# Two of the five subtractions that make wv's low parts: on VectorE instead of GpSimd, with the written-out order of TensorE's products made anew

## The chip, the core and the metric

The kernel runs on one core of a Trainium2 chip. The metric is the device time of one execution in microseconds, as the median of several runs. Before the change it is 1871.93 us (three runs, 1871.77 to 1875.42).

## The reference

x is 2048 rows of 640 numbers, float32 throughout. The output is the sum of x, an attention block and a token-mixing MLP, both fed with the layer norm of x:

```python
xn = layernorm(x)
qkv = xn @ wqkv                      # 32 heads of 20
o = softmax(q @ k.T * 20 ** -0.5) @ v
A = o @ wo
h = gelu(layernorm(xn) @ w1)         # then shifted by +1, -1, +2, -2 rows, a quarter of the columns each
x1 = xn + shifted(h) @ w2
B = x1 + gelu(layernorm(x1) @ w3) @ w4
out = x + A + B
```

## The kernel before, in words

**Numbers in two parts.** To keep float32 precision on TensorE, an operand is split into a high part (a rounded copy in the fp32r type) and a low part (the operand minus its high part). A product is three: high by high, high by low, low by high. The high part is a copy, mostly on ScalarE; the low part is a subtraction, on GpSimd or VectorE. A pair of such products that uses the two 64-row halves of the array side by side is called twins here; between the first and the second half of a twin sum stands a fence, a one-element memset of `scratch` on GpSimd, which waits for the last product of the first half and releases the first of the second.

**The first stage** (to about 30 us) loads x in 16 tiles (`xb`), takes the mean and variance of each on VectorE (`bn_a`, `mva`), works out the norm's factors in short steps on GpSimd (`rv_a` is VectorE's, then `rn_a`, `ry_a` which is the power -0.5, `rt_a`, and `lnk` at the end), scales the tiles (`xb` again, on VectorE and ScalarE in turn), transposes them on TensorE (`tp`) and splits the result into `xT` (high copy on ScalarE, low subtraction on VectorE). Tiles go in groups: 0 and 1, 2 and 3, then 4 to 7, 8 to 11, 12 to 15. For each block of four tiles the products with the first 128 columns of the q and k weights (`w_q`, `w_k`, sums named `ps`) follow, their split `hl`, and a placing product `pk`. The first half of the v weights (`wv`, five pieces of 128 x 320, one per 128 rows) and `w_k`, `w_q` (128 x 640 each) are split in the same stretch. Their subtractions are tied behind the scaling of tile 2 on VectorE. After the five pieces of wv, GpSimd has the subtractions of `w_k` and `w_q`, four memsets of the buffers `vst` (which held the raw v weights), and the norm factors of the next block.

**After the first stage** the attention (maxima `pm` and `mx`, scores `s`, exponentials `p`, weighted sums `pv`) runs through the whole kernel, and the dense products (v, q, k, w1 to w4, wo) fill in between.

**What sets the order.** The program lists operations with keys (smaller is more urgent) and costs; a planner walks through them in modelled time and emits one order for each engine. The engines then work in that order. For TensorE the kinds are written out in the string `ORDER` of 7059 letters: m a maximum step, s a score step, p a weighted sum, d anything else; which d comes is still chosen by key. Operations marked `port=True` are kept apart in the plan: no such operation of VectorE overlaps one of GpSimd there. That holds in the modelled time alone; on the chip only the order on each engine and the waits for data stand.

Nearly all vector, scalar and GpSimd instructions are recorded at L324 (the line in `Plan.__call__` that issues them), products at L356, fences at L344.

Of the kernel before, what the change touches and what calls it, by code (L numbers as in the profile page):

```python
# [97 lines left out]
ORDER = (  # L98
    "dddddddddddddddddddddddddddddddddddddddddddddddddddddddddddddddddddddddddddddddddddddddddddddddddddddddddmmddd"
    "ddddddddddddddddddddddddddddddddddddddddddddddddddddddddddddmdddddddmddddmddddmddddmddddddmdddddddddddddddmddd"  # L100
    "dddmmdddddddmdddddmddddddddmdmddddddddddddddddddmdddddddddmdmmdddddddddddddddmdddddddddddmddddmmdddddddddddddd"
    "mdddddmddddddddmdddmmdddddddddddddddddddddmddddddddmdmmdddddddmddddddddddddddddddddmddmddmdddddddmdddddddddddd"
    "mdddddddddddsmmdddddddddddsddsdddddddsdmdddddddddmssddddddddmdsdddsdddmdddddsdmdsddppppddmsddmddsdmdsddsddmdds"
    "dddsdmdmddppppmddddmsdddsddddmdsdddsmdddsdmdsddddsmddsddmddmmppppmdsdddsdsdmdddmdsddmdddsmddddsdmddsdmddsddmdm"
    "ddmdpppsmspsmsmspmsmpsmspmsmpsmssmpmsmpsmddddsmddddmdddsdmdddsmdddsdmdddsdmddsdmddmddsppssmpsmmppmdddsddmddsdd"
    "dmddddmdspddmsdddddsdmdsdddddmddmppsmddddddddsmdddddddsmdddddsddmdddsddddmdmppmsdddddsddmdsddddmdddsmddddddsdm"
    "ddddsdddmdmppppsmddddsddmddsddddsdddmsddddddmsddddmdddddsmpmsmpppdsmdddsddddddmsdddddsmddddsddmddsdddmdddmdspp"
    "ppdmdsmdddddddsddmdddddmsddddddmsdddsdddmdddmppsdmdddddsdmddddsddmddsdmdddsdddmddsdddddmdmppsmdddddsdmddsddddd"
    "ddmsmdddddddsddddmddmddmppmsmppmdsdsdddmdsddddmsdddddmmsdddddddmsdddsddmsdddsppmspsmsddpdssmpdddppsddsddmdddsd"
    "ddsdmddddsmdddmddsdddmddsddmdddsppmmspppdmsddddmsdddsdmdsdddddmsmdddsdddmdsddsdddmddmdsppmsmsppmsdddmmpdpdsmdd"  # L110
    "ddmdsdddmddsddmddsdmdsdddmdsdddsddmddsddspsmpmspdmspdppdmdsddmddddmddddsdddsmddsddmddsdddsmdsddmddsdmppppmsddm"
    "dddddmsdddmdsdmdddsmddddmsdddmddsdmdddsddmppsmmppmsddddsdsmddddsdmddsdddmsddmddsdmdddspsmpsdmdddmdsddddsmppdmm"
    "sdpdpsdddsdsdddddmsddddsdddmsddddmdsddddmdsdddmddsppmmsmspppsmspsmddddmdsdmdddmddsddddmsdddmsddddmsdddmdsdddmd"
    "mppssppsmdddddpssmpmdddsdmdddsdmdddsddddsmddddmdsdddmdddsddsddmpppmsmpdddsmddddmddmddsdddddmsddddmdsddddmsdddd"
    "ddsmsmpsmpppsmspsddmdpmdsddmdsdddmsdddddmssdddddmddmdsddsddmddsdpsmmpppsdmddddsmdsdddmdsddmddsdsppppmsdddmsddd"
    "msdddmdsddmdddssdddddpsmmppmddsdmddmdddddsdmpdmsdddsdmsdddmdsddmddsdmdddsddsdmppppmsdddmdsddsddsdmddddddmsmddd"
    "ddddsmddddmsddsddmsmmpppmspsmspsmddddsmdddsdmpsmddddmddsdmdsddddmspsdmpsmdddsdddmsddsdmdddddmddsppppddsmddsddm"
    "dddsmddsddmdsdmddsddmdsdmddmdmppppssddmddddmsdddmdsdddddmsmddddsddmdddsmdddsddmdmppppmsddmdsdddmdsddmddsddmdds"
    "mdddmdsdddsdsddmpsmpsmpsmpmsddmdsddddsdddsdmdmdpppdsddmddsdddsmpmsddmdsddmdsdddsddmsdddmdsppsmmppmsdddmdsddmdd"
    "ddmdsddddmsmdddddsmddddmdsdddmddspsmmpppmdddmddsdddmsddddmsdddmsddmdsdddmddmsddddsdmddspmspssmpsmspsmsdpsmspms"  # L120
    "mpmspssmpssmpssmpmsspsmpssmpsmmppmsddddmddddmdddddddmmdddddsdddddddddddddddmsddsddddddddssdddmddddddmdsdddddsd"
    "dddmdmppppmdddsdddddddsmdmddddddsddmddddsdddddddddddddddsddddddddddddmsmddddddsddddmddddddddsddmddddddmddddspp"
    "ppdmdsddddsddddmsddddsdddddddddddddsdddddsdddmsddddddmmdddddddsdddmdddmddppdsppmdddddsdmddsddddddsmdsddddddsdd"
    "mdddddsdmppsdmddddddsdmdddddsddmpdmsddddddmddsddddddmspsmpsmspssmppsddddddddddddddddddddsspmmspsmmppmmddsddddd"
    "dmdddmsddddsmdmddddddmsdddmdsdddmddddmdsddmdddmsdddmddddsmddddmdsdmddddspppppmsdddddddmddsddmddsddmddsdddsmddd"
    "sddmddsddsddmddddmmppppmsdddmdddddsdmddsdmdddsmdddsdmdddsdmdddsdmdddsmpppmsdddsdmdsdddmdsdddmsdddsmdsddddmmppp"
    "msdpsmddsddmdsddmddsdmpppsmdddsdmdddsdmdddsdmdddsmdddsdmddsdmddsdmddsdddmmppppmdddmddddsddmddsddddssdddmdddsds"
    "ddmdddsddsdspppsmspmmsppsmdddsdmdddsdmdddsdmdddsmdddsdmdddsddmddsdddmdspdppmsddmdsdddmsddmdsddmdsdddmmppppmsdd"
    "sddmdsdddmdsdmdddsdddddmddddmmdddddddsmdppsdmdddsdmddsddsddmdddsdmpsmspssmppppmsddmdsddddmsdmdddsddmddsmdddsdm"
    "ddddsmddsddmdddmsppppdmdsdmdddsdmdddmdsdddddssmdddddsddmddsdmdddddsmmmppmpmmspsmspsmspsmspsmspsmspsmspssmpmsmp"  # L130
    "ddddsmdddmdddsdddddsmdddsdddmddmppsmdddddddddddsdddsdddmdddddsmddddddddsdddmddddddddsdddddmdddspmddsdpdsmdsddd"
    "ddddmddddmmdddddddddddddpppddmdddddddsddddddsmddddddmddddmdddddspsmdddsddddmddsddsddddmsdddddmddsdddmdddsddddd"
    "dddddddppppmsdddddmsddddsdmdddddsmdddddmsdddmddddddmdspmsppddmsdddddddmsddddddsdmddddddsdmddddddmdspdmdsddmddd"
    "ddsddddddmmdddddsddddddsddddmsppdmsmppsmspssmpmsspmsspmsddddddddssddddddddddddpmspssmpsmspsmspsmspsmdddddsspps"
    "sddddmdsddddmdmmddddddmdddmdddddddddmdddddmdddddddmsdddmdddmddddmdsddmdddddmddmddddmdsdddddmmddddsddmddsdppdmd"
    "dsddddmmpppmddsddmdddddmddsdmdddsmdddsdmddsdmddsdmddsddmdsppsmspppsmdddsdmdddsdmdddsdmdddsmdddsddmddsddmddsdds"
    "ddmpppssmpppmsddsddmddsddmddsdmddddsmdsdddmddsdmddddsmddddmsppppddmdmdddsddddsdmdsddddmsddmddsdsddddmsdddmdmdd"
# [448 lines left out]
def c_act(n, psum=True):  # L586
    return n * 0.8333 + (50.0 if psum else 93.0)
# [6 lines left out]
def c_pool(n):  # L594
    return 2.11 * n + 145.0
# [6 lines left out]
def _f(v):  # L602
    return v.bitcast(F32)


def tile_kernel(tc, x, wqkv, wo, w1, w2, w3, w4, out):
    nc = tc.nc
    pl = Plan(tc)
# [192 lines left out]
    wvs, nbs, rvs = [], [], []  # L801
# [17 lines left out]
    def v_load(h):  # L819
        vp = pl.pool(name=f"vw{h}", bufs=1, side="right")  # L820
        w = vp.tile([P, 2, ND, 320], F32R, name=f"wv{h}")
        for k in range(ND if h else 0):
            load_row(w, "v1", k, 1)
        return vp, w
# [4 lines left out]
    vw0 = v_load(0)  # L829
    vst = [vsp.tile([P, 8, 2, VC], F32, name=f"vst{i}") for i in range(VSB)]  # L830
    wvr = [v.rearrange("p a b c -> p (a b c)")[:, :320] for v in vst]
# [9 lines left out]
    def split_wv():  # L841
        k, pl.key = pl.key, -903.0
        for i in range(ND):
            pl("act", c_act(320, False), "copy", vw0[1][:, 0, i, :], wvr[i])
            wvs.append(pl("pool", c_pool(320), "tensor_sub", vw0[1][:, 1, i, :], wvr[i], _f(vw0[1][:, 0, i, :]), port=True))
        pl.key = k

    pl.key = -140.0
# [2 lines left out]
    def norm_rows(ts):  # L851
# [30 lines left out]
        if ts[0] == 0:  # L882
            split_wv()
# [681 lines left out]
```

## Time and profile before

| | |
|---|---|
| median of three runs | 1871.93 us (1871.77 to 1875.42) |
| the profiled execution's own time | 1870.62 us |
| its span, first to last instruction | 1868.5 us |
| TensorE busy | 1855.8 us, 99% of the span |
| VectorE busy | 1550.7 us, 83% |
| ScalarE busy | 1337.8 us, 72% |
| GpSimd busy | 404.8 us, 22% |
| granted TensorE clock, mean | 0.999 |

The profiled execution lies 2.1 us above its span and 1.3 us below the median. In the tables PE is TensorE's products, PEld its weight loads, DVE is VectorE, ACT is ScalarE, POOL is GpSimd. Busy time is an average over stages; what an edit in one stage is worth is read from that stage.

### The profile page before, as it was taken

Reading aid. Unit: us, or ns where it says so; the run is one execution under the profiler, and the core shown is the slowest. Engines: PE = TensorE matmul, PEld = TensorE weight load, DVE = VectorE, ACT = ScalarE, POOL = GpSimd, SP = SyncE. Lnnn points to the kernel's source line nnn. Section 1 sums busy time; section 2 is a strip of 40 time slices with the busy share of each in tenths; the row PEclk is TensorE's granted clock in tenths of the full one; section 3 lists DMA queues with packets and bytes.
Section 4 is the critical chain, followed back from the end, with each engine's and each line's share of the span. In section 5 each row is a group of like instructions: output and inputs, shape, how many; then the busy total and the mean of one; then the engine's idle time right before and its main releaser. Section 6 shows DMA issues by size and latency. Waiting matters only on the chain.

```text
span 1868.5 us, 44324 instructions
## 1 busy us (share of the span) xinstructions
PE 1855.8 (99%) x17233; PEld 1276.6 (68%) x17233; DVE 1550.7 (83%) x2739; ACT 1337.8 (72%) x2459; POOL 404.8 (22%) x620
## 2 busy tenths in 40 slices
PE   9999999999999999999999999999999999999998
PEld 7975776666666648676666756665776777775777
DVE  8989888888888999988788988778887888789724
ACT  5267777787877886677887677788677777778661
POOL 6001111321212213211213320111222122212211
PEclk9999999999999999999999999999999999999999
DMA  5664555536353475645345673434423242343402
GB/s 200 178 184 134 136 136 158 162 115 180 107 158 122 123 243 169 189 151 177 118 127 187 210 208 102 126 98 151 121 80 91 73 116 84 81 135 121 139 13 113
DMA packets 230360, 257.79 MB, mean 138 GB/s; under 512 B 60520, under 2 KB 175672, under 8 KB 228352
## 3 DMA queue, kind: packets, MB, share of 16 engines
q1 hardware_dynamic: 230152, 254.98, 45.7%
q8 instruction: 135, 2.21, 0.5%
q14 instruction: 73, 0.60, 0.1%
HBM read 151.64 MB, written 103.25 MB: 136 GB/s over the span
## 4 chain that ended last, share of the span: by engine, by line
PE 95%; DVE 2%; POOL 1%; DMA 1%; issue 0%; SPq 0%; ACT 0%; DVEq 0%; POOLq 0%; ACTq 0%
PE ps L356 26%; PE pv L356 25%; PE s L356 14%; PE pm L356 14%; PE psv L356 4%; PE pso L356 3%; PE ps_k L356 3%; PE ps_q L356 3%; DVE mx L324 1%; PE psl L356 1%; PE tz L324 1%; DMA wd_w<-ph_w 0%; PE pmt L356 0%; PE c_w L356 0%; PE tp L324 0%
## 5 line engine op out<-in xcount | busy, mean ns | idle before, releaser
L324 DVE TENSOR_REDUCE mx<-pm 128x1 f32<-128x512 f32 x2048 | 1282.2, 683 | 207.9 <-PE pm L356 192.9
L324 ACT ACTIVATE p<-s 128x512 f32<-128x512 f32 x2048 | 1080.8, 611 | 277.4 <-PE s L356 232.7
L356 PE MATMUL pv<-p,v 128*32 128x512 f32 x4096 | 493.7, 598 | 0.1
L356 PE MATMUL s<-zq,kpack 62*128 62x512 f32 x2048 | 443.4, 410 | 0.7
L356 PE MATMUL pm<-kpack,zq 60*128 60x512 f32 x2048 | 441.0, 409 | 1.6 <-DVE ob L324 1.6
L356 PE MATMUL ps<-xT,w_w 64*128 64x512 f32 x2040 | 322.8, 394 | 0.4 <-DVE mx L324 0.3
L356 PEld LDWEIGHTS s<-zq,kpack 62*128 62x128 f32 x2048 | 227.4, 185 | 128.2 <-ACT p L324 38.6
L356 PEld LDWEIGHTS pm<-kpack,zq 60*128 60x128 f32 x2048 | 228.3, 185 | 110.6 <-DVE mx L324 26.3
L356 PEld LDWEIGHTS pv<-p,v 128*32 128x32 f32 x4096 | 110.2, 109 | 225.0 <-issue 196.1
L356 PEld LDWEIGHTS ps<-xT,w_w 64*128 64x128 f32 x2040 | 212.9, 186 | 32.9 <-issue 2.1
L324 POOL TENSOR_TENSOR ob<-ob,obq 128x512 f32<-128x512 f32 x96 | 125.2, 1304 | 403.2 <-ACT obq L324 312.3
L356 PE MATMUL ps<-xT 64*128 64x320 f32 x1632 | 168.0, 307 | 0.0
L356 PEld LDWEIGHTS ps<-xT 64*128 64x128 f32 x1632 | 150.2, 186 | 9.0 <-issue 2.5
L356 PE MATMUL ps<-xT,gT 64*128 64x320 f32 x1152 | 119.1, 307 | 0.0
L324 ACT COPY obq<-pv 128x512 f32<-128x512 f32 x75 | 44.1, 588 | 103.8 <-PE pv L356 102.8
L356 PEld LDWEIGHTS ps<-xT,gT 64*128 64x128 f32 x1152 | 104.4, 186 | 6.2 <-issue 0.8
L344 POOL MEMSET scratch<- 1x1 f32 x134 | 12.1, 90 | 432.0 <-PE ps L356 206.3
L356 PE MATMUL psv<-wv,xT 64*128 64x320 f32 x960 | 92.1, 309 | 1.0 <-ACT xT L324 0.8
L356 PEld LDWEIGHTS psv<-wv,xT 64*128 64x128 f32 x960 | 80.9, 185 | 7.4 <-POOL scratch L344 1.2
L356 PE MATMUL ps_q<-xT,w_q 64*128 64x512 f32 x480 | 77.9, 393 | 0.0
L356 PE MATMUL ps_k<-xT,w_k 64*128 64x512 f32 x480 | 74.4, 394 | 0.0
L324 POOL TENSOR_TENSOR ph_w<-pr_w,ph_w 128x320 fp32r<-128x320 f32 (+2 forms) x48 | 36.7, 764 | 151.6 <-ACT ph_w L324 120.9
(171 smaller groups left out, 1360.9 us busy)
## 6 DMA issues: line engine op xcount, KB each, us to landing
zq<-qd SPq DMA_DIRECT2D x156, 80.0 KB
kpack<-kd SPq DMA_DIRECT2D x78, 160.0 KB
w_w<-wd_w SPq DMA_DIRECT2D x48, 256.0 KB
gd<-pre SPq DMA_DIRECT2D x8, 1536.0 KB
g<-gd SPq DMA_DIRECT2D x64, 192.0 KB
wd_w<-ph_w SPq DMA_DIRECT2D x34, 320.0 KB
xT<-wd_w SPq DMA_DIRECT2D x34, 320.0 KB
vd<-vst SPq DMA_DIRECT2D x32, 256.0 KB
```

The costliest lines, as they stand in the source:

```text
L324: o.insts = [getattr(e, m)(val(out), *[val(x) for x in ins], **{k: val(v) for k, v in kw.items()})]
L344: o.insts = [nc.gpsimd.memset(scratch.get(), 0.0)]
L356: o.insts = [nc.tensor.matmul(out.get(), lhsT.get(), rhs.get(), **kw) for out, lhsT, rhs, kw in products]
```

## The change

In `split_wv`, which lists the five copies and five subtractions for wv's parts, the subtractions of pieces 2 and 4 are now listed for VectorE, with VectorE's cost in the planner; pieces 0, 1 and 3 stay on GpSimd. Key, tie and marking are as before. None of the five may be moved to another engine by the planner. The string ORDER is another one of the same length with the same number of each letter. Counted letter by letter, 77 of its 1024 m, 78 of its 1024 s and 11 of its 512 p stand elsewhere, by 23 places at most, in 32 stretches; the first 232 letters are the same. The core of the diff:

```diff
--- before
+++ after
@@ -98,40 +98,40 @@
 ORDER = (
...
-    "dddmmdddddddmdddddmddddddddmdmddddddddddddddddddmdddddddddmdmmdddddddddddddddmdddddddddddmddddmmdddddddddddddd"
-    "mdddddmddddddddmdddmmdddddddddddddddddddddmddddddddmdmmdddddddmddddddddddddddddddddmddmddmdddddddmdddddddddddd"
-    "mdddddddddddsmmdddddddddddsddsdddddddsdmdddddddddmssddddddddmdsdddsdddmdddddsdmdsddppppddmsddmddsdmdsddsddmdds"
-    "dddsdmdmddppppmddddmsdddsddddmdsdddsmdddsdmdsddddsmddsddmddmmppppmdsdddsdsdmdddmdsddmdddsmddddsdmddsdmddsddmdm"
-    "ddmdsdddmddsddmddsdmdsdddmdsdddsddmddsddspsmpmspdmspdppdmdsddmddddmddddsdddsmddsddmddsdddsmdsddmddsdmppppmsddm"
-    "dddddmsdddmdsdmdddsmddddmsdddmddsdmdddsddmppsmmppmsddddsdsmddddsdmddsdddmsddmddsdmdddspsmpsdmdddmdsddddsmppdmm"
+    "dddmmddddddddmddddmdddddmddddmddddddddddddddddddmdmdddddddddmmddddddddddddddmddddddddddddmddddmmdddddddddddddd"
+    "mdddddmddddddddmdddmmddddddddddddddddddddddmdddmdddddmmddddddddddddmdddddddddddddddmdddmdddddddmdddddddddddddm"
+    "ddddmdddddddsmddddmddddddsddsddddddddsddsdmdddddddmsddddsddmdddsdddmdddddsdmppppdsddsdddmdmdddsddmsdddsddddmds"
+    "dddsdmdmddppppmddddmdsddsdddsdmddddsmddsdddmsddddsmddsddmddmmppppdmsddsddsdmdddmdsdmddddsmddddsdmddsdmddsddmdm"
+    "ddmdsdddmddsddmddsdmdsdddmdsdddsddmddsddspsmpmspdmspdppdmdsddmddddmddddsdddsmddddsmddsdddsmdsddmddsdmppppmsddm"
+    "ddddmsdddmdsddmdddsmddddmdsddmddsdmdddsddmppsmmppmsddddsdsmddddsdmddsdddmsddmddsdmdddspsmpsdmdddmdsddddsmppdmm"
...
@@ -842,7 +842,9 @@
         k, pl.key = pl.key, -903.0
         for i in range(ND):
             pl("act", c_act(320, False), "copy", vw0[1][:, 0, i, :], wvr[i])
-            wvs.append(pl("pool", c_pool(320), "tensor_sub", vw0[1][:, 1, i, :], wvr[i], _f(vw0[1][:, 0, i, :]), port=True))
+            on = i in (2, 4)
+            wvs.append(pl("dve" if on else "pool", (c_dve if on else c_pool)(320), "tensor_sub", vw0[1][:, 1, i, :], wvr[i],
+                          _f(vw0[1][:, 0, i, :]), port=True))
         pl.key = k
 
     pl.key = -140.0
```

## Rows read from the trace of the kernel before

**Rows 1.** The page, part 1: busy time and share of the span, by engine.

```profile
PE 1855.8 (99%) x17233; PEld 1276.6 (68%) x17233; DVE 1550.7 (83%) x2739; ACT 1337.8 (72%) x2459; POOL 404.8 (22%) x620
```

**Rows 2.** Stretches: from:to, length, busy us and instructions by engine, clock, DMA share, GB/s.

```profile
10.00:30.00 20.00, 17.41 (x141) 13.27 (x141) 18.56 (x49) 12.02 (x23) 14.42 (x31) 1.00 0.67 249
30.00:60.00 30.00, 30.00 (x240) 24.75 (x238) 27.22 (x56) 12.36 (x23) 6.20 (x13) 1.00 0.33 111
```

**Rows 3.** Chain that ended last, 0 to 160 us: start us, us, what.

```profile
...
13.37 2.56 POOL wv L324 x3
15.93 1.54 POOL w_k L324
17.47 1.50 POOL w_q L324
...
19.61 0.97 POOL ry_a L324
...
23.96 0.91 ACT xb L324
...
25.49 1.29 DVE hl L324 x2
26.78 1.80 DVE xT L324 x3
28.63 3.71 PE ps L356 x29
...
```

**Rows 4.** GpSimd in order of time: start us, us, instruction, idle before it.

```profile
...
11.71 3.40 POOL L324 TENSOR_TENSOR wv<-vst,wv 128x320 fp32r<-128x320 f32 x4 [0.51 <-ACT xT L324]
...
20.98 0.09 POOL L344 MEMSET scratch<- 1x1 f32 x1
...
22.90 0.20 POOL L324 TENSOR_TENSOR lnk<-rn_a,lnk 128x4 f32<-128x4 f32 x1
23.05 1.30 POOL L324 TENSOR_TENSOR ry_a<-rv_a,mhalf 128x4 f32<-128x4 f32 x1
...
25.55 0.20 POOL L324 TENSOR_TENSOR lnk<-rn_a,lnk 128x4 f32<-128x4 f32 x1
...
```

**Rows 5.** VectorE in order of time, 10.9 to 19 us.

```profile
...
11.49 1.62 DVE L324 TENSOR_TENSOR xT<-tp,xT 128x512 fp32r<-128x512 f32 x3
...
18.77 0.22 DVE L324 SCALAR_TENSOR_TENSOR rv_a<-mva 128x4 f32<-128x4 f32 x1
...
```

**Rows 6.** TensorE in order of time: its two waits for GpSimd after 18 us.

```profile
...
19.03 0.50 PE L356 MATMUL ps<-xT,w_q 64*128 64x512 f32 x1 [0.81 <-POOL w_q L324]
...
21.13 0.50 PE L356 MATMUL ps<-xT,w_q 64*128 64x512 f32 x1 [0.68 <-POOL scratch L344]
...
```

**Rows 7.** VectorE, groups by form: busy us, mean ns, idle before.

```profile
...
L324 DVE TENSOR_TENSOR ph_w<-pr_w,ph_w 128x320 fp32r<-128x320 f32 x10 | 4.9, 490 | 0.9 <-ACT ph_w L324 0.7
...
```

**Rows 8.** Both engines in order of time, two places late in the kernel.

```profile
...
1786.66 0.68 DVE L324 TENSOR_TENSOR oT<-oc,oT 128x512 fp32r<-128x512 f32 x1
...
1786.82 1.67 POOL L324 TENSOR_TENSOR oT<-oc,oT 128x512 fp32r<-128x512 f32 x1 [4.30 <-DVE oT L324]
...
1817.44 1.30 POOL L324 TENSOR_TENSOR ob<-ob,obq 128x512 f32<-128x512 f32 x1 [5.54 <-ACT obq L324]
...
1818.11 1.18 DVE L324 TENSOR_TENSOR oTl<-oc,oTl 128x512 fp32r<-128x512 f32 x1
...
1831.88 0.69 DVE L324 TENSOR_TENSOR oTl<-oc,oTl 128x512 fp32r<-128x512 f32 x1
...
```

**Rows 9.** Chain that ended last, where TensorE changes to weighted sums and back.

```profile
...
107.66 3.57 PE pv L356 x32
...
156.57 1.00 PE pv L356 x8
157.56 0.42 PE pm L356 x2
158.22 0.24 PE pm L356 x2
...
```

More of the change, by code (lines that the diff above doesn't have):

```diff
@@ L110 @@
     "ddsdmddddsmdddmddsdddmddsddmdddsppmmspppdmsddddmsdddsdmdsdddddmsmdddsdddmdsddsdddmddmdsppmsmsppmsdddmmpdpdsmdd"
-    "ddmdsdddmddsddmddsdmdsdddmdsdddsddmddsddspsmpmspdmspdppdmdsddmddddmddddsdddsmddsddmddsdddsmdsddmddsdmppppmsddm"
-    "dddddmsdddmdsdmdddsmddddmsdddmddsdmdddsddmppsmmppmsddddsdsmddddsdmddsdddmsddmddsdmdddspsmpsdmdddmdsddddsmppdmm"
+    "ddmdsdddmddsddmddsdmdsdddmdsdddsddmddsddspsmpmspdmspdppdmdsddmddddmddddsdddsmddddsmddsdddsmdsddmddsdmppppmsddm"
+    "ddddmsdddmdsddmdddsmddddmdsddmddsdmdddsddmppsmmppmsddddsdsmddddsdmddsdddmsddmddsdmdddspsmpsdmdddmdsddddsmppdmm"
     "sdpdpsdddsdsdddddmsddddsdddmsddddmdsddddmdsdddmddsppmmsmspppsmspsmddddmdsdmdddmddsddddmsdddmsddddmsdddmdsdddmd"
-    "mppssppsmdddddpssmpmdddsdmdddsdmdddsddddsmddddmdsdddmdddsddsddmpppmsmpdddsmddddmddmddsdddddmsddddmdsddddmsdddd"
-    "ddsmsmpsmpppsmspsddmdpmdsddmdsdddmsdddddmssdddddmddmdsddsddmddsdpsmmpppsdmddddsmdsdddmdsddmddsdsppppmsdddmsddd"
+    "mppssppsmdddddpssmpmdddsdmdddsdmdddsddddsmddddmdsdddmdddsddsddmpppmsmpdddsmddddmddmddsdddddmsddddmddsdddmddsdd"
+    "ddsmsmpmspppsmspsdddmdpmsddmdsddmdsdddddsmsdddddmdmddsdddsdmddsdpsmmpppsdmdddsdmdsdddmdsddmddsdsppppmsdddmsddd"
     "msdddmdsddmdddssdddddpsmmppmddsdmddmdddddsdmpdmsdddsdmsdddmdsddmddsdmdddsddsdmppppmsdddmdsddsddsdmddddddmsmddd"
-    "ddddsmddddmsddsddmsmmpppmspsmspsmddddsmdddsdmpsmddddmddsdmdsddddmspsdmpsmdddsdddmsddsdmdddddmddsppppddsmddsddm"
+    "ddsmddddddmsdsdddsmmmpppmspsmspsmddddsmddddsmpsmddddmdsddmdsdddmdspsmpmsdddsdmdsdddddsmdddddmdsdppppdsmddddsdm"
     "dddsmddsddmdsdmddsddmdsdmddmdmppppssddmddddmsdddmdsdddddmsmddddsddmdddsmdddsddmdmppppmsddmdsdddmdsddmddsddmdds"
@@ L120 @@
     "ddmdsddddmsmdddddsmddddmdsdddmddspsmmpppmdddmddsdddmsddddmsdddmsddmdsdddmddmsddddsdmddspmspssmpsmspsmsdpsmspms"
[L121 to L125, printed above, removed]
+    "spmspssmpssmpssmpmsmpsmpssmpsmmppmsddddmddmdddddddddmmddddddsddddddddddddmdsdddsdddddmdddssdddddddddmdsdsddddd"
+    "ddmddmppppmsdddddddddmdsddsdddmddddmddddsdddddddddddddddsddddddddddddmsmddddddsddddmddddddddsddmddddddmddddspp"
+    "ppdmdsddddsddddmsdddddsdddddddddddsddddddsdddsmddddddmmdddsdddddddmddddmdpppmspsmddddddddsdddddddssmddddddddsd"
+    "mdddddmdsppsdmdddddsdmdddddddmdspmdsdddddmdddsddddddmspsmpsmspssmppsmddddddddddddddddddddspsmspsmmppmmddsddddd"
+    "mddddmsddddsmdmddddddmsdddmdsdddmddddmdsddmdddmsdddmddddsmddddmdsdmddddspppppmsdddddddmddsddmddsddmddsdddsmddd"
     "sddmddsddsddmddddmmppppmsdddmdddddsdmddsdmdddsmdddsdmdddsdmdddsdmdddsmpppmsdddsdmdsdddmdsdddmsdddsmdsddddmmppp"
@@ L130 @@
     "ddddsmddsddmdddmsppppdmdsdmdddsdmdddmdsdddddssmdddddsddmddsdmdddddsmmmppmpmmspsmspsmspsmspsmspsmspsmspssmpmsmp"
[L131 to L134, printed above, removed]
+    "ddddsmdddmdddsdddddsmdddsdddmddmppsmdddddddddddsdddsdddmdddddsmdddddddsdmdddddddddddsddddddddmspmdsddpdsmddsdd"
+    "dddmdddmdmddddpddddddddddppdddddmddddsddddddsmddddddmddddmdddddspsmdddsddddmddsddsddddmsdddddmddsdddmdddddsddd"
+    "dddddddppppmsdddddmsddddmdsdddddmsdddddmsddddmddsdddmdpmppsdddmsdddddmsdddddddsmdddddddsdmddddddmdspdmdsddmddd"
+    "ddsddddddmmdddddsddddddsddddmsppdmsmppsmspssmpmspsmsspmsddddddddssddddddddddddpmspssmpsmspsmspsmspsmdddddsspps"
     "sddddmdsddddmdmmddddddmdddmdddddddddmdddddmdddddddmsdddmdddmddddmdsddmdddddmddmddddmdsdddddmmddddsddmddsdppdmd"
```

## The prediction, made before the changed kernel ran

> **What bounds the kernel now.** I read the page first, then the stretches, then the chain of waits, and last each engine in order of time between 10 and 30 us. The page [rows 1] shows TensorE busy for 1855.8 of 1868.5 us: 12.7 us of idle time in all are what any better order could win back. The stretches [rows 2] show where the changed operations stand: from 10 to 30 us TensorE works 17.41 us and waits 2.59, and from 30 to 60 us it has no idle time. So the edit acts in a short stage in which TensorE waits for others; what that stage gains or loses by about 28.6 us is carried to the end, because TensorE is full behind it.
>
> The chain [rows 3] shows who sets that stage. It runs through GpSimd: wv's subtractions (the last ends at 15.93), w_k's (1.54 us), w_q's (1.50, to 18.97), then the power for the next block's norm (19.61), then ScalarE's scaling of its tiles (23.96), VectorE's subtractions for hl and xT (25.49 to 28.58), and TensorE from 28.63 on. The two waits of TensorE that GpSimd causes are 0.81 us for w_q's low part and 0.68 us for a fence [rows 6]; the fence itself was done only after 20.98 us, behind the power and a memset in GpSimd's queue [rows 4]. Together 1.49 us.
>
> **The change part by part.**
>
> *Removed from GpSimd:* two of five subtractions of 128 x 320. The first four begin at 11.71 and the fifth ends as w_k's starts, at 15.93 in the chain [rows 3, 4]: 4.22 us for five, 0.84 each, 1.69 for two. If nothing else happened, w_k's subtraction would begin 1.69 us earlier and w_q's would end at 17.28 instead of 18.97.
>
> *Added to VectorE:* two subtractions of the same form. The nearest rows are ten subtractions of 128 x 320 with both operands in SBUF, 490 ns each [rows 7]; 0.98 us for two. VectorE is already busy for 18.56 of these 20 us [rows 2], so nearly all of it delays something there.
>
> *Do the two engines work side by side?* Two places late in the kernel answer that [rows 8]. At 1818.11 VectorE began a subtraction with two operands in SBUF while GpSimd had been in an addition since 1817.44, to 1818.74. It took 1.18 us; the same form alone takes 0.69. It ended 0.55 us after GpSimd had. At 1786.82 GpSimd began one while VectorE was in such a subtraction to 1787.34; it took 1.67 us, where 1.30 is its length at 1817.44. So whoever comes second waits for the first, in both directions. The sum goes by that: of the 1.69 us taken off GpSimd, two VectorE subtractions of 0.49 come back as waits, and 0.71 remain. w_q's low part would be there at 18.26 instead of 18.97, and of the wait of 0.81 us before 19.03, 0.71 go.
>
> The Trainium skill ("SBUF — State Buffer", section "Who interferes with whom") states this as a rule: a VectorE instruction with two SBUF inputs contends with a GpSimd instruction that reads SBUF, and the later of the two fully blocks. The two places above agree with it (0.49 and 0.37 us of lengthening). Without the rule GpSimd's gain would be the whole 1.69 us, which is the second rival below.
>
> *What VectorE's own delay does.* After the scaling of tile 2 VectorE makes three low parts of xT from 11.49 to 13.11 [rows 5], then statistics. The moved subtractions stand behind their own ScalarE copies and behind the scaling of tile 2, so they can run from 11.6 us; I expect them after those three low parts, because the planner keeps them apart from GpSimd's. Each finds GpSimd inside a subtraction of 0.84 us: the wait is between 0 and 0.84, on average 0.42. VectorE loses 2 x (0.49 + 0.42) = 1.82 us; the bounds are 0.98 and, if each has to wait for one of the long subtractions of w_k and w_q instead, 0.98 + 1.54 + 1.50 = 4.02. Queued behind them are the statistics of tiles 4 to 7 and `rv_a`, which ended at 18.99 [rows 5]; it is followed by the power on GpSimd, which began at 19.61 in the chain [rows 3]. With 1.82 us of delay `rv_a` ends at 20.81 and the power begins then, 1.20 later than before.
>
> *What is given back behind it.* In the kernel before, GpSimd's steps from this power to the factors ran from 19.61 to 23.10, 3.49 us, because memsets of vst stand between them; the next block's steps, with nothing between, ran from 23.05 to 25.75, 2.70 us [rows 3, 4]. With GpSimd free earlier and waiting for `rv_a`, those memsets fall into its idle time. The factors would be there at 20.81 + 2.70 = 23.51 instead of 23.10: 0.4 us late. At the lower bound for VectorE's delay it is 19.97 + 2.70 = 22.67, 0.4 early; at the upper, 23.01 + 2.70 = 25.71, 2.6 late.
>
> *The sum of the stage.* On the path through w_q, 0.71 us are gained, on that through the factors, 0.4 lost, and the two meet at about 24 us, where the first block's sums end and the next block's transposes begin. The fence's 0.68 us wait can go either way: it goes if its memset now stands before the power, and grows if it stands behind a later one. I take the middle of +0.4 and -0.7, rounded: -0.1 us. Its bounds are -1.5 (both waits gone) and +2.6.
>
> *The order string.* The written-out order moves no work in or out. By the letters the runs of p go from 258 to 259. A change back from weighted sums to maxima shows as 0.42 us for a pair where the next takes 0.24, and a run of eight products takes 1.00 where four such in a row take 3.57, so 0.89 each [rows 9]: one more run costs 0.18 + 0.11 = 0.3 us. The rest are swaps of neighbours in 32 stretches, with no row that prices them. Below, they could win what idle time is left outside 10 to 30 us, 12.7 - 2.6 = 10.1 us; above, a product put in front of an operand that is late costs a wait like the ones of 0.68 and 0.81 [rows 6], in the 32 stretches at most 32 x 0.81 = 26 us. Nearly all places are swaps of a few letters within work that is ready, so I take 0 for them, and keep a tail on both sides.
>
> Altogether -0.1 + 0.3 = +0.2 us on the profiled execution's 1870.62, thus 1870.8. That execution lies 1.3 us under the median, so against the median it is 1872.1.
>
> **The rivals.**
>
> *The engines work side by side after all* (GpSimd's operands are other tiles than VectorE's). GpSimd is free 1.69 us earlier, both waits of TensorE go, -1.5 + 0.3 = -1.2: 1870.7 us. Against it stand both places of [rows 8]; for it, that the two engines' subtractions may by luck not meet.
>
> *VectorE gets stuck behind the long ones* (slower). If the moved subtractions come to VectorE's head when GpSimd has turned to w_k and w_q, each waits for one of 1.5 us, `rv_a` ends at 23.01 and the factors are 2.6 us late: +2.6 + 0.3, 1874.8 us. It decides from a VectorE delay of 1.4 us on (18.99 + 1.4 + 2.70 = 23.1, the time of before); the forecast's 1.8 is already past that. For it: the planner's separation in modelled time puts them late. Against it: VectorE can put off statistics of later tiles to let `rv_a` through. Even this stays under 0.2%.
>
> *The new order is better or worse as a whole.* Some of the 32 stretches take idle time away, or put TensorE before late operands. Only this could move the time by more than 0.2% (3.7 us, about what a measurement of this kernel can tell from no change): five more waits of the size of [rows 6], or as many fewer; 1868 or 1876 us. For it: the idle time outside the stage is 10.1 us. Against it: TensorE is full around most of these places, and equal amounts of work change seats.
>
> That the two subtractions stay on GpSimd is excluded: the listing gives them VectorE and no alternative.
>
> **How the numbers follow.** Forecast, stage and order near neutral: 0.45, at 1872.1. Side by side: 0.13. Stuck: 0.14. Order better by over 0.2%: 0.16; worse by over 0.2%: 0.12. The first three lie within 0.2%: 0.72; faster 0.16, slower 0.12. The range must reach to the edges of the last two, and the runs of before themselves reach from 1871.77 to 1875.42: 1867.4 to 1876.2. The middle case alone lies between 1870.5 (-1.5) and 1874.8 (+2.6).
>
> **What would show it.** GpSimd: three subtractions of wv before w_k's, and w_q's low part done between 17.3 and 18.3 us. VectorE: two subtractions of wv lasting more than 0.49 us, or GpSimd's beside them more than 0.84. `rv_a` of tiles 4 to 7 later than 18.99, the power following it at once, and no memsets inside the steps to `lnk`. TensorE's wait for w_q below 0.2 us. The products that begin at 28.63 begin within one or two microseconds of that. If the end moves by more than the stage did, the order is the cause. The prediction is wrong if a stretch behind 60 us gains or loses more than 3 us of TensorE time.

## The result, and the profile of the changed kernel

The changed kernel takes 1876.3 us (median of 20 runs, 1873.38 to 1885.39) against 1873.22 for the kernel before, timed in turn with it on the same chip. The ratio is 1.0022, with a 95% interval of 1.0014 to 1.0030: about 3 to 4 us slower. The prediction was 1872.1 us, 0.2 above the 1871.93 that it took for the kernel before; its range ended at 1876.2. Of the 4.2 us between forecast and result, 1.3 are the kernel before itself, which measured 1873.22 here.

The profiled execution of the changed kernel took 1883.2 us (span 1881.1), 7 us above the median of its own runs, so its last microseconds are not those of a usual run. A second profile of the same kernel, from the experiments (e3), has a span of 1871.4; its execution took 1873.59 us, 3 us below the median of its own runs. Where the two differ, both are given. Part 1 of the page, to be held against [rows 1]:

```profile
PE 1862.9 (99%) x17233; PEld 1279.9 (68%) x17233; DVE 1554.6 (83%) x2746; ACT 1337.2 (71%) x2457; POOL 400.5 (21%) x615
```

TensorE has the same number of products and is "busy" 7.1 us longer, so the page cannot say where the time went: short waits between products and stretches at a lower clock count as busy time (two examples below: a pair of products that lasts 0.99 us instead of 0.41, and the place near 1102 us). The stretches, with the columns of [rows 2]:

```profile
10.00:30.00 20.00, 17.33 (x137) 12.79 (x137) 18.48 (x46) 11.32 (x23) 13.14 (x30) 1.00 0.64 236
30.00:60.00 30.00, 29.17 (x224) 23.33 (x222) 26.36 (x56) 13.37 (x24) 5.84 (x13) 1.00 0.32 112
```

GpSimd works 13.14 us from 10 to 30 where it worked 14.42, but TensorE is no busier there, and from 30 to 60 us it now has 0.83 us of idle time where it had none. GpSimd in order of time, to be held against [rows 4] and the chain in [rows 3]:

```profile
12.19 2.54 POOL L324 TENSOR_TENSOR wv<-vst,wv 128x320 fp32r<-128x320 f32 x3 [0.51 <-ACT xT L324]
14.69 1.56 POOL L324 TENSOR_TENSOR w_k<-wr_k,w_k 128x640 fp32r<-128x640 f32 x1
16.19 0.53 POOL L324 MEMSET vst<- 128x512 f32 x1
16.68 1.56 POOL L324 TENSOR_TENSOR w_q<-wr_q,w_q 128x640 fp32r<-128x640 f32 x1
18.18 1.45 POOL L324 MEMSET vst<- 128x512 f32 x3
21.30 0.20 POOL L324 TENSOR_SCALAR rn_a<-mva 128x4 f32<-128x4 f32 x1 [1.67 <-DVE mva L324]
21.43 0.09 POOL L344 MEMSET scratch<- 1x1 f32 x1
21.71 1.01 POOL L324 TENSOR_TENSOR ry_a<-rv_a,mhalf 128x4 f32<-128x4 f32 x1 [0.19 <-DVE rv_a L324]
...
```

VectorE in order of time, to be held against [rows 5]:

```profile
16.29 0.47 DVE L324 TENSOR_TENSOR wv<-vst,wv 128x320 fp32r<-128x320 f32 x1
16.68 1.91 DVE L324 TENSOR_TENSOR wv<-wvr,wv 128x320 fp32r<-128x320 f32 x1
...
21.48 0.14 DVE L324 SCALAR_TENSOR_TENSOR rv_a<-mva 128x4 f32<-128x4 f32 x1
...
```

The first moved subtraction met a memset and took 0.47 us. The second began in the same hundredth of a microsecond as GpSimd's for w_q, which ended at 18.24, and lasted 1.91 us, to 18.59. `rv_a` begins 2.7 us later than before (21.48 against 18.77), and GpSimd stands idle for 1.67 us until VectorE's statistics (`mva`) come. TensorE's waits, against [rows 6]:

```profile
15.54 0.49 PE L356 MATMUL ps<-xT,w_q 64*128 64x512 f32 x1 [0.18 <-ACT w_q L324]
...
18.64 0.42 PE L356 MATMUL psv<-wv,xT 64*128 64x320 f32 x2 [0.24 <-DVE wv L324]
...
21.58 0.50 PE L356 MATMUL ps<-xT,w_q 64*128 64x512 f32 x1 [1.39 <-POOL scratch L344]
```

The wait of 0.81 us for w_q's low part is gone, as forecast (the 0.18 is for ScalarE's high copy). The wait for the fence has doubled, from 0.68 to 1.39: its memset now stands behind `rn_a`, which waits for VectorE's late statistics.

**Lateness by position.** ScalarE works the same exponentials in the same order in every kernel here, so the k-th one can be compared between two traces. The numbers are its start less that of the same one in the profile of before, worked out from the traces; the heads are the time in before. A difference between two columns is what a stretch lost; the last column is near the end.

| profile | 95 | 312 | 369 | 1017 | 1072 | 1098 | 1128 | 1834 |
|---|---|---|---|---|---|---|---|---|
| changed kernel | 3.2 | 3.5 | 3.5 | 4.6 | 6.1 | 6.8 | 11.5 | 12.9 |
| changed kernel, second profile (e3) | 2.5 | 2.4 | 0.9 | 0.2 | 1.7 | 2.3 | 2.7 | 3.2 |

Two things repeat in these two: 2.5 to 3.2 us are lost by 95 us, and 2.1 to 2.2 us between 1017 and 1098 us, far from the edited lines. The rest differs from one execution to the next: the second profile gets 1.5 us back at 331 us, where TensorE waits for VectorE and a store anyway; the first loses 4.7 us between 1098 and 1128. The experiments take these apart.

### The profile page after: what moved, and what is told of

It reads as the page before. It is cut to its first block, busy times and chain, and to the rows that moved or that the text cites. A ratio compares the mean times of both kernels' runs of the same rounds, so it can differ in the third digit from the quotient of the medians.

```text
span 1881.1 us, 44327 instructions
## 1 busy us (share of the span) xinstructions
PE 1862.9 (99%) x17233; PEld 1279.9 (68%) x17233; DVE 1554.6 (83%) x2746; ACT 1337.2 (71%) x2457; POOL 400.5 (21%) x615
```

## The experiments

Each kernel was timed in five rounds, in turn with the kernel before on the same chip; ratios are to the kernel before. "Old" and "new order" are the strings ORDER of before and after.

**The two parts by themselves.** e1: the changed code with the old order. e2: the code of before with the new order. e3 and e5: the changed kernel and the kernel before once more, as a measure of what repeats.

```diff
     # e1: split_wv as changed, ORDER as before
     # e2: split_wv as before, ORDER as changed
```

> The two subtractions on VectorE, with the order string of before. Theory A (VectorE is the loss: 0.98 us of added work plus about 1.4 us in which its second subtraction stands behind GpSimd's w_q subtraction, carried through the statistics of the later tiles): most of the loss is here, +2.5 to +4 us against before, the second subtraction about 1.9 us long, TensorE at the same score step near 150 us later by 2 to 3 us. Theory B (the new order string is the loss): within 1 us of before.

> All five subtractions on GpSimd, with the new order string. Theory A: within 1.5 us of before, the first 30 us as before. Theory B: +3 to +4 us.

> The changed kernel once more, to tell what repeats in its trace from what one execution did. Both theories: +3 to +5 us in the median. Theory A: some 3 us late by 150 us in the trace again; the lateness that the first trace gathered between 1070 and 1130 us (some 6 us) is of that one execution and is gone or elsewhere. Theory B: it gathers in the stretches where the order differs, 350 to 400 and 690 to 770 and 1060 to 1130 us.

> The kernel before once more: how far two sets of runs of one program lie apart, and whether its 1.5 us wait near 331 us and its undisturbed stretch from 1060 to 1130 us repeat. Every theory: a ratio of 1.000 within 0.001; a trace within 1 us of the first one at 150 us and within 2 us at the end.

Measured: e1 1.0014 (0.9998 to 1.0030), e2 1.0017 (1.0006 to 1.0028), e3 1.0017 (1.0006 to 1.0027), e5 0.9997 (0.9985 to 1.0010). The order alone is slower by as much as the whole change. e1 was left open by its interval (one of its 12 runs took 1889.92 us), so it was timed again (e12):

> The changed code with the old order, a second time, since the first interval (0.9998 to 1.003) left it open. If the first stage's lateness is carried to the end: 1.5 to 2.5 us above before, ratio 1.001. If most of it is given back where TensorE waits for transfers anyway (near 331 us): at most 1 us, ratio 1.0000 to 1.0005, as with the five added statistics.

e12: 1.0004 (0.9993 to 1.0015). The code part is within the measurement of no change, though both results together (about 1.0007, give or take 0.0009) leave room for up to 3 us. Its profiles are 1.5 (e1) and 2.9 us (e12) late at 95 us. What differs between them is which engine blocked the other. In e1, VectorE and GpSimd in order of time:

```profile
16.82 0.49 DVE L324 TENSOR_TENSOR wv<-wvr,wv 128x320 fp32r<-128x320 f32 x1
...
16.84 1.91 POOL L324 TENSOR_TENSOR w_q<-wr_q,w_q 128x640 fp32r<-128x640 f32 x1
```

and in e12:

```profile
16.83 1.92 DVE L324 TENSOR_TENSOR wv<-wvr,wv 128x320 fp32r<-128x320 f32 x1
...
16.82 1.58 POOL L324 TENSOR_TENSOR w_q<-wr_q,w_q 128x640 fp32r<-128x640 f32 x1
```

The same code; the two starts lie 0.01 to 0.02 us apart, VectorE ahead in e1 and behind in e12, and 1.4 us of VectorE time hang on that. The recorded starts do not decide it alone: in e15 (below), with the same subtractions, VectorE's starts 0.01 us behind and takes 0.48 us, GpSimd's 1.91. VectorE was the one delayed in both profiles of the changed kernel, e10 and e12, GpSimd in e1, e7 and e15.

**Where the early lateness arises.** The column at 95 us holds two steps, which TensorE's products with w_q, taken one by one like the exponentials, show apart. At 28.63 us, where the prediction ended its stage, they are 0.6 to 1.1 us late where VectorE was the one delayed (1.0 in the changed kernel, 0.6 in e3), and 0.2 to 0.9 us early where GpSimd was (e1 0.3). Between 36 and 43 us all seven lose another 1.8 us. There VectorE scales the last tiles of x; before had both of its scalings ahead of `hl` and `xT`, e1 has the second behind them:

```profile
34.90 1.13 DVE L324 TENSOR_SCALAR xb<-xb,mva,lnk 128x640 f32<-128x640 f32 x2
```

```profile
41.34 0.61 DVE L324 TENSOR_SCALAR xb<-xb,mva,lnk 128x640 f32<-128x640 f32 x1
```

and TensorE's transposes in e1 wait for it, where before has no wait (a further 0.21 us at 40.28, for `xT`; the rest of the 1.8 does not show as a wait):

```profile
42.00 1.53 PE L324 MATMUL tp<-ident,xb 128*128 128x128 f32 x12 [0.46 <-DVE xb L324]
```

e4, e6, e8 and e11 below lose 1.7 to 1.8 us at the same place, so this step does not hang on the two engines blocking each other; no run takes it apart further.

**What lateness early on is worth.** e6: the kernel before with five idle statistics on VectorE (their results are not used), placed as the moved subtractions are.

```diff
+            sx = lnp.tile([P, 2, 6], F32, tag="bnx", name=f"bnx{i}")
+            xs.append(pl("dve", 402.0, "bn_stats", sx[:, 0, :], wvr[i]))
...
-                for o in {0: wvs[:WVE], 2: wvs[WVE:] + w0s}.get(t, ()):
+                for o in {0: wvs[:WVE], 2: wvs[WVE:] + w0s + xs}.get(t, ()):
```

> The kernel before, with five extra statistics instructions of 0.44 us on VectorE (2.2 us, one SBUF input each, so no meeting with GpSimd) tied behind the scaling of tile 2; their results are not used. Theory A (VectorE's time in the first stage is what the two subtractions cost): rv_a of tiles 4 to 7 and of tiles 12 to 15 later by 1.5 to 2.2 us, 1.5 to 2.5 us late at 95 us, +1.5 to +2.5 us in all. Rival (the loss comes from GpSimd's changed queue or from the order string): less than 0.5 us late at 95 us.

Measured: 1.0001 (0.9989 to 1.0013). The profile is 2.7 us late at 95 us, 1.6 at 395, 0.5 at 1017 and 0.3 early at the end: lateness of this kind can be absorbed at later waits for transfers.

**Keeping the two engines apart.** e4 (new order) and e11 (old order): w_k's and w_q's subtractions tied behind the last of wv's, so that VectorE's two can meet only short ones.

```diff
-                    pl.behind(o, nx)
+                    pl.behind(o, wvs[4] if o in w0s else nx)
```

> The changed kernel, but GpSimd's subtractions of w_k and w_q are tied behind VectorE's second subtraction of wv, so that VectorE can't stand behind a 1.5 us one. Theory A: both VectorE subtractions under 1.4 us, rv_a of tiles 4 to 7 earlier by 0.7 to 1.5 us than in the changed kernel, and 1 to 2 us of the 4 come back. Theory B: no change against the changed kernel, +3 to +4 us.

> The changed code with the old order, and with the subtractions of w_k and w_q tied behind the last of wv's, so that VectorE's two meet only short ones. Theory A (the first stage's loss is the lock behind w_q): about 0.5 us each for VectorE's two subtractions, at 95 us at most 1 us later than before, and a median within 1 us of before, ratio 0.9995 to 1.0005. Rival (VectorE's added millisecond share is the loss, wherever its two stand): 1.5 to 2.5 us late at 95 us as in the code alone, ratio about 1.001. Rival (the moved subtractions free GpSimd and gain once unlocked): 0.5 to 1.5 us under before.

In e11 VectorE's two take 0.48 us each:

```profile
14.60 0.48 DVE L324 TENSOR_TENSOR wv<-vst,wv 128x320 fp32r<-128x320 f32 x1
14.99 0.48 DVE L324 TENSOR_TENSOR wv<-wvr,wv 128x320 fp32r<-128x320 f32 x1
...
19.77 0.14 DVE L324 SCALAR_TENSOR_TENSOR rv_a<-mva 128x4 f32<-128x4 f32 x1
```

`rv_a` comes 1.7 us earlier than in the changed kernel, but the fence's wait stays at 0.91 us (18.77 brings one of 0.38 for w_q back), and e11 is 2.1 us late at 95: more than the 1 us expected. The times are e4 1.0015 (1.0005 to 1.0025) and e11 1.0004 (0.9991 to 1.0016): with the new order the loss stays, with the old there is none to measure. So the engines do block each other, and that is not the loss.

**Other repairs.** e8: the kernel before with the memsets of vst held behind the norm factors of tiles 4 to 7, so that these come earlier; e7: the changed kernel with wo's high copies on GpSimd, away from VectorE's queue near 1102 us.

```diff
-        pl("pool", 500.0, "memset", v, 1.0).deps.append((wvs[-1], 0))
+        pl("pool", 500.0, "memset", v, 1.0).deps += [(wvs[-1], 0), (nbs[2], 0)]
...
+        elif name[:2] == "wo":
+            pl("pool", c_pool(n), "tensor_copy", hl[:, 0, :n], raw[:, :n], port=True)
```

> The kernel before, all five subtractions on GpSimd, with the four memsets of vst held back until the norm factors of tiles 4 to 7 are done. Theory A says that GpSimd's part of the first stage is better mended here: the factors of tiles 4 to 7 at about 22.3 instead of 23.10 us, the fence's wait of 0.68 us gone, 0.5 to 1 us early at 95 us, -0.5 to -1 us in all. Rival (the rest of the stage hangs on VectorE): less than 0.3 us at 95 us.

> The changed kernel, with the high copies of wo's pieces on GpSimd instead of VectorE, so that none of them can hold VectorE while it waits for the store of the piece before. Theory C (in the new order such a copy stands in front of an evacuation that TensorE needs near 1102 us, and what it costs depends on how late the store is, 0 to 4.5 us): no wait of TensorE over 0.5 us between 1095 and 1115 us, no lower clock behind it, 1 to 2 us less in the median than the changed kernel and fewer runs above 1878. Rival (the waits there come from the shared queue of transfers as such): TensorE waits there as before, for another instruction.

Neither gained: e8 1.0009 (0.9996 to 1.0021), e7 1.0020 (1.0010 to 1.0030). In e8 the factors were done at 22.17 us and the fence's wait fell to 0.21, but the next power came at 26.38 instead of 23.05, after GpSimd, its memsets done at 24.04, had stood idle for 1.93 us until VectorE's statistics came; TensorE waited 1.04 us for VectorE's `hl` at 27.9, and the profile was 3.4 us late at 95 us and 4.8 at the end, where 0.5 to 1 us early was expected. In e7 the wait near 1102 was gone and the loss from 1017 to 1098 was 3.6 us instead of 2.2.

**Where in the order.** Between 1017 and 1098 us every profile so far with the new order lost 2.1 us or more (e15, below, 1.9), and none with the old lost over 0.1. e9: the kernel before with only letters 3580 to 3910 (products from about 1016 to 1090 us; 42 of the letters differ) taken from the new order; e16 the same again. e10: the reverse, the changed kernel with those letters from the old.

```diff
     # e9, e16: code of before, ORDER = old[:3580] + new[3580:3910] + old[3910:]
     # e10: changed code,       ORDER = new[:3580] + old[3580:3910] + new[3910:]
```

> Code of before and its order, but for 330 letters of it (positions 3580 to 3910, products that run from about 1016 to 1090 us), which come from the new order. Theory B (the order's steady loss sits in this stretch: 2.3 us between 1059 and 1084 us in every profile with the new order, at most 0.1 in those with the old): the same loss of about 2.3 us between 1059 and 1084 here, and a median 2 to 4 us above before, ratio 1.001 to 1.002. Rival (the order's cost is scattered over its 32 stretches, or comes from the first stage): no loss in that stretch, and less than 1 us in all.

> The changed kernel, but with those same 330 letters taken back from the old order. Theory B: no loss between 1059 and 1084 us, no copy of ph_wo in front of the evacuation near 1102, and a median 0 to 1.5 us above before, ratio 1.0000 to 1.0008. Rival (scattered, or the first stage): 3 to 4 us above before as the whole change, 1.0015 to 1.0022.

> The 330 new letters alone, a second time, beside the two above on the same chip: 1.0012 as before if that was the letters and not chance, within 0.0004 to 1.0021; about 2 us lost between 1059 and 1084 us and a wait for the loaded maxima (zq) behind it, between 0.3 and 1.5 us.

e9: 1.0012 (1.0004 to 1.0021). e16: 1.0007 (0.9998 to 1.0016). e10: 1.0002 (0.9992 to 1.0013). Much of the loss goes with these letters: without them the changed kernel cannot be told from before. e9 and e16 together give about 1.0010, the whole new order (e2) 1.0017; whether the other letters hold the rest is not shown. Lateness as above:

| profile | 1017 | 1059 | 1072 | 1084 | 1098 | 1128 |
|---|---|---|---|---|---|---|
| e9, letters alone | 0.1 | 0.8 | 1.7 | 3.7 | 4.9 | 5.2 |
| e16, the same again | -0.6 | 0.0 | 0.9 | 1.7 | 1.5 | 7.0 |
| e10, all but the letters | 3.4 | 3.3 | 3.3 | 3.3 | 3.2 | 4.3 |
| e13, letters, copy on ScalarE | 0.7 | 1.3 | 2.2 | 3.5 | 3.3 | 4.3 |
| e17, letters, rb behind the fence | -1.7 | -1.1 | -0.6 | 2.0 | 2.0 | 2.4 |
| e18, letters, both | -0.8 | -0.1 | -0.2 | 1.4 | 1.8 | 2.2 |
| e14, old order, copy on VectorE | 1.3 | 1.3 | 1.8 | 5.7 | 9.0 | 9.4 |

The two expectations of a loss between 1059 and 1084 us hold in e9 (2.9) and e16 (1.7), and the place is right; the ratio of e16 alone would not have shown it. Another 0.6 to 0.7 us are lost between 1017 and 1059 in every row with the new letters; some of that is only that the letters place these exponentials elsewhere, and no run takes it apart.

**What the letters do there.** The string names only TensorE's kinds, but the planner walks on from it, and the order on other engines comes out differently, in two places here and on SyncE's queue further below. One is GpSimd's order at a fence; the kernel before, GpSimd in order of time:

```profile
1061.63 0.09 POOL L344 MEMSET scratch<- 1x1 f32 x1 [1.94 <-PE s L356]
...
1069.90 0.09 POOL L344 MEMSET scratch<- 1x1 f32 x1 [0.24 <-PE ps L356]
...
1077.27 1.31 POOL L324 TENSOR_TENSOR rb<-ob,rb 128x512 f32<-128x512 f32 x1
```

and e9:

```profile
1062.30 0.38 POOL L344 MEMSET scratch<- 1x1 f32 x1 [2.26 <-PE s L356]
...
1070.30 1.32 POOL L324 TENSOR_TENSOR rb<-ob,rb 128x512 f32<-128x512 f32 x1
1071.53 0.09 POOL L344 MEMSET scratch<- 1x1 f32 x1
```

A multiplication for another block (`rb`, 1.3 us) that stood 7 us behind the fence now stands in front of it, and TensorE's next sums wait for that fence. The other is a copy: of a finished weighted sum (`obq`), 0.59 us on ScalarE at 1066.48 in before, 0.68 us on VectorE at 1067.38 in e9, in a stretch in which VectorE has no idle time and the maxima queue behind it; TensorE's pair of maxima products that lasts 0.41 us in before (1067.51) lasts 0.99 in e9 (1068.22). The copy was put back, `rb` was moved behind the fence, each by itself and both together (e13, e17, e18), and the copy was put on VectorE in the kernel before (e14); e15 is e13's edit in the whole changed kernel.

```diff
     # e13, e15 ("act", c_act, "copy"); e14 ("dve", c_dve, "tensor_copy")
-            evac(part, pvs[blk], 512)
+            if (blk, qt) == (17, 1):
+                pl("act", c_act(512), "copy", part, pvs[blk], dk=K_FE)
+            else:
+                evac(part, pvs[blk], 512)
     # e17, and in e18 with the above: rb of block 16 after T of block 18
+        o = pl("pool", 150.0, "tensor_sub", T[:, :, 1, :], nm, _f(hr))
+        if blk == 18:
+            rbs[16].deps.append((o, 1))
```

> The kernel with the 330 new letters, but the copy of block 17's second quarter (obq, 128 x 512) held on ScalarE as in the kernel before. If the copy is the cause: VectorE has no obq near 1067 us, the maxima come 0.6 to 0.7 us earlier from there, and the loss between 1059 and 1084 us shrinks from 2.0 to under 1.4 us; if the copy is all of it, to under 0.5, and the median is within 1 us of before. Rival (the letters' places cost by themselves): 2 us or more lost as with the letters alone, ratio 1.001.

> The kernel before with its own order, and only that copy moved from ScalarE to VectorE. If the copy is the cause: TensorE's maxima wait between 1066 and 1075 us, 0.6 to 2 us are lost between 1059 and 1084, and the maxima's way through DRAM to the next scores is late too; ratio 1.0003 to 1.001. Rival: no loss there, ratio 1.0000.

> The whole changed kernel with that copy held on ScalarE. If the copy is the cause: as the changed kernel with the old letters there, ratio 1.0002 to 1.001, and under 1.4 us lost between 1059 and 1084. Rival: as the changed kernel, 1.0015 to 1.0022.

> The 330 new letters, with GpSimd's multiplication of block 16 (rb) held behind the short steps for block 18's maxima, so behind the fence near 1071 us; the copy of the weighted sum stays on VectorE. If the multiplication in front of the fence is the steady loss: the fence is done 0.7 to 1.2 us earlier relative to its sums, and the loss from 1059 to 1084 us falls from 2 to about 1 us; the maxima's load may still be late. Rival (the letters themselves): 2 us or more as before.

> Both at once: the multiplication behind the fence and the copy on ScalarE. If the two share the loss (whichever is later sets the fence or the maxima): no fence wait over 0.2 us near 1072, at most 1 us lost between 1059 and 1084, and a median within 1 us of before, ratio 0.9995 to 1.0005. Rival (the letters themselves): 2 us as with the copy alone, ratio 1.0004 to 1.001.

Measured: e13 1.0004 (0.9995 to 1.0013), e14 1.0033 (1.0022 to 1.0045), e15 1.0019 (1.0008 to 1.0029), e17 1.0017 (1.0005 to 1.0028), e18 1.0008 (0.9995 to 1.0021).

By the traces the copy alone is not the loss under the new letters: e13 loses 2.2 us from 1059 to 1084 and e15 is as slow as the changed kernel (e13's own time is nearer to before than that of e9 and e16, but the intervals overlap). With the copy off VectorE it is the fence that TensorE waits for; e13, TensorE in order of time:

```profile
1072.29 0.99 PE L356 MATMUL ps<-xT,hs 64*128 64x320 f32 x10 [0.78 <-POOL scratch L344]
...
1086.89 0.66 PE L356 MATMUL s<-zq,kpack 62*128 62x512 f32 x2 [0.77 <-DMA zq<-md]
```

With `rb` moved as well (e18) the fence is done before it is wanted, and from 1059 to 1072 us nothing is lost any more (-0.1, where e9, e13 and e16 lose 0.9); with `rb` alone (e17) it is 0.5. So that part, 0.9 us, is the fence and the copy together. But e18 then loses 1.6 us by 1084 (e17 loses 3.1 from 1059 to 1084, where 1 was expected), in the wait for the two halves of one load:

```profile
1084.79 0.47 PE L356 MATMUL s<-zq,kpack 62*128 62x512 f32 x1 [1.05 <-DMA zq<-md]
1085.87 0.47 PE L356 MATMUL s<-zq,kpack 62*128 62x512 f32 x1 [0.61 <-DMA zq<-md]
```

These are the first scores of block 18. Their maxima go from VectorE (`mT`) to DRAM (`md`) and back (`zq`), and in before TensorE does not wait for this round trip. SyncE's queue in before:

```profile
1076.05 0.31 SPq L324 DMA_DIRECT2D md<-mT  x1
1076.46 1.73 SPq L324 DMA_DIRECT2D xT<-wd_w  x2
1078.61 1.02 SPq L324 DMA_DIRECT2D onm<-rb  x3
1080.94 0.52 SPq L324 DMA_DIRECT2D zq<-md  x2
```

in e18:

```profile
1075.83 0.33 SPq L324 DMA_DIRECT2D md<-mT  x1
1076.26 1.42 SPq L324 DMA_DIRECT2D onm<-rb  x4
1077.78 3.92 SPq L324 DMA_DIRECT2D xT<-wd_w  x3
1081.74 0.75 SPq L324 DMA_DIRECT2D zq<-md  x2
```

and in e14:

```profile
1078.15 0.31 SPq L324 DMA_DIRECT2D md<-mT  x1
1078.51 0.52 SPq L324 DMA_DIRECT2D xT<-wd_w  x1
1080.12 3.09 SPq L324 DMA_DIRECT2D onm<-rb  x4
1083.82 1.40 SPq L324 DMA_DIRECT2D xT<-wd_w  x2
1085.26 0.75 SPq L324 DMA_DIRECT2D zq<-md  x2
```

In e18 the maxima leave 0.2 us earlier than in before and their load is issued 0.8 us later, with the four stores of `rb` (`onm`) and three larger loads between. That is in part the repair's own doing, for `rb` stands behind the fence now but not where before had it (1077.27):

```profile
1074.00 1.29 POOL L324 TENSOR_TENSOR rb<-ob,rb 128x512 f32<-128x512 f32 x1
```

In e9, e13 and e16, without that repair, no such store stands between, and from store to load it is 4.9 to 5.0 us, as in before (4.9; e17 5.5, e18 5.9, e14 7.1). Their waits for `zq` (1.46, 0.77 and 0.32 us) come behind that: from the load's issue to its first use it is 2.9 to 4.3 us in e9, e13, e16, e17, e18 and e14, and 1.8 without a wait in before. What makes the load itself longer was not tested. In e14, which is 1.3 us late already at 1059, the maxima leave 2.1 us later and the load 4.3 us later. TensorE in e14, and the stretches around:

```profile
1088.72 0.95 PE L356 MATMUL s<-zq,kpack 62*128 62x512 f32 x2 [3.90 <-DMA zq<-md]
```

```profile
1085.00:1090.00 5.00, 1.27 (x6) 0.67 (x10) 1.96 (x4) 1.46 (x4) 0.00 (x0) 0.84 0.91 297
1090.00:1100.00 10.00, 10.00 (x60) 4.22 (x53) 6.18 (x12) 6.85 (x16) 1.51 (x2) 0.74 0.77 175
```

With one copy of 0.68 us listed for the other engine, and the queues planned anew behind it, TensorE waits 3.9 us, has a granted clock of 0.74 for the next 10 us, and loses 7.7 us from 1059 to 1098. That is the largest effect of any run here, with no letter changed.

**The place near 1102 us.** What differs most between executions is here. e16, VectorE in order of time:

```profile
1101.89 0.33 DVE L324 CAST ph_wo<-pr_wo 128x320 fp32r<-128x320 f32 x1 [3.65 <-DMA wd_wo<-ph_wo]
1102.13 0.68 DVE L324 COPY ob<-pv 128x512 f32<-128x512 f32 x1
```

A copy for wo, which waits for an earlier store of its buffer, stands in front of the evacuation that TensorE needs; TensorE waited 2.81 us at 1102.87, and the granted clock from 1100 to 1110 was 0.83: 5.5 us from 1098 to 1128. In the first profile of the changed kernel the wait was 2.58 us (clock 0.90), in the second none. It is no mark of the new order: e11, with the old, waited 1.95 us for VectorE there, e1 0.71, before and e12 not at all.

## Why the prediction was wrong

*The order string* is the step that failed: "Nearly all places are swaps of a few letters within work that is ready, so I take 0 for them". The order alone measured 1.0017, some 3 us, and the 330 letters of one of its stretches 1.0012 and 1.0007. The letters themselves are swaps of neighbours; what they move is the planner's choices behind them on engines that the string does not name: by the traces GpSimd's `rb` in front of a fence and VectorE for a copy in place of ScalarE (0.9 us together); the load `zq` also comes late (0.3 to 1.5 us of waiting in e9, e13 and e16), and that SyncE's order does this is not shown. The prediction looked at TensorE's side alone. Its rival "the new order is worse as a whole" had the right size (1876 us) and a chance of 0.12; its mechanism, more waits of the size of [rows 6], is what happened, in one stretch and not in many.

*The mark that the prediction set* ("if the end moves by more than the stage did, the order is the cause") pointed the right way: the second profile was 0.6 us late at 28.63 us, 2.5 at 95, 0.2 at 1017 and 3.2 at the end.

*GpSimd's gain* was right in size: three subtractions in 2.54 us, w_q's low part done at 18.24 (18.26 forecast), its wait gone. The way was another: the forecast had VectorE's two come back on GpSimd as waits, and in both profiles of the changed kernel GpSimd did not wait; a memset of vst and a stage that ran 0.5 us later took the place, so the agreement is in part luck.

*The two engines block each other*, as the prediction had it from [rows 8]: 1.91 us for a VectorE subtraction of 0.49, or 1.91 for GpSimd's of 1.56, one of the two in every meeting. This is the rule of the Trainium skill ("SBUF — State Buffer", "Who interferes with whom"), and the trace agrees with it here as well.

*VectorE's delay* was mis-sized: 1.82 us with bounds to 4.02; `rv_a` measured 2.7 us late in the changed kernel (some 0.5 of it because the whole stage ran later there from the first tiles of x on), 2.35 in the second profile. The "stuck" rival happened for one subtraction of the two. At 28.63 us the stage was not 0.1 us early but 0.6 to 1.0 late, within the forecast's bounds; with GpSimd the one delayed (e1, e7, e15) it was 0.2 to 0.9 early.

*That this would reach the end* ("TensorE is full behind it") was wrong twice. Between 36 and 43 us, in the stretch that [rows 2] shows without idle time, another 1.8 us were lost: TensorE was full there only as long as VectorE's scalings of x came in time. And later most of it was given back: e6 and e12 show 2.7 and 2.9 us of lateness at 95 us and 1.0001 and 1.0004 in time. At 331 us TensorE waited 1.55 us in before for an evacuation behind a copy that waits for a store; a late TensorE waits less there (0.2 in e12). Not in every execution: the first profile of the changed kernel kept its 3.5 us (it waited 1.71 there), and e8 and e10 kept theirs.

**What stays open.** The intervals of e9, e13, e16, e17 and e18 overlap; that the fence, the copy and the load each cost time is read from the traces, not from the times, and no version was found that beats the kernel before. e18's 1.0008 also lies where its rival, that the letters cost by themselves, had put it. Whether another order of SyncE's queue would save e18's last 1.6 us was not tried, nor was the first fence's longer memset (below) undone by itself.

## What to carry to other kernels

A written-out order for one engine is an input to the plan of all the others. Before costing a reshuffle at nothing, list what changed on every queue (who does each copy, what stands in front of each fence and each small load), above all where an engine is full or the next work waits for a round trip through DRAM. A stretch without idle time is full only as long as its suppliers come in time. Lateness in an early stage is worth only what no later wait for a transfer takes back: compare the same instruction at several places of two traces before believing that it is carried to the end.

## What the runs showed of the hardware that was not expected

A one-element memset can take four times as long beside VectorE. The fence's at 1062.30 in e9 took 0.38 us, where the one at 1061.63 in before took 0.09. VectorE in order of time, e9:

```profile
1062.04 1.13 DVE L324 TENSOR_SCALAR x<-x,mv,ry_c 128x640 f32<-128x640 f32 x2
```

and before:

```profile
1061.56 1.13 DVE L324 TENSOR_SCALAR x<-x,mv,ry_c 128x640 f32<-128x640 f32 x2
```

The memset came 0.26 us after VectorE's start in e9, and ended (1062.68) with the first of the two scalings (1062.65); in before it came 0.07 us after. In ten of the eleven profiles with the new letters here it came 0.25 to 0.26 us after VectorE's start and took 0.38 us; in all nine with the old letters it came 0.07 to 0.09 us after and took 0.09; in e7 it came before VectorE and took 0.09. That is seen at this one place and was not tested by itself.

Which of two engines that start within 0.01 us of each other goes on and which takes 1.9 us changed between two executions of one kernel (e1 and e12), and e15 shows that the recorded start does not tell. The same short wait can be followed by a lower granted clock or not: after 0.68 us at 21.13 the kernel before kept 1.00; after 0.69 us at 21.20, with the same products, e2 had 0.85 from 20 to 22 us, then 0.50 (the lower level) from 22 to 24:

```profile
22.00:24.00 2.00, 2.00 (x12) 1.57 (x10) 1.80 (x6) 0.82 (x1) 1.92 (x6) 0.50 0.00 0
```

and its pairs came every 0.42 us instead of 0.23. That is nearly all of the 1.8 us by which e2, whose code there is that of before, is late at 95 us; e13 had the same. What decides it is not in the trace.
